# A planned kernel is planned anew: other model constants, five instead of six float32 heads kept, another order

## Chip, core and metric

The kernel runs on one core of a Trainium2 chip. The core has five engines with a queue of instructions each, worked off in order: PE (TensorE, matrix products into PSUM), DVE (VectorE), ACT (ScalarE), POOL (GpSimd) and SP (SyncE, which here only issues transfers). The metric is the time of one execution on the device in microseconds; of several runs the median counts.

## What is computed

Attention in hash buckets, and a feed-forward layer on its output. The reference, cut:

```python
# q, k, v: (4, 8, 768, 64) float32; proj: (64, 6)
q_bucket = np.sum(q_bits * powers, axis=-1)      # q_bits = (q @ proj > 0), k the same
mask = q_bucket[:, :, :, None] == k_bucket[:, :, None, :]
scores = scale * np.matmul(q, k.transpose(0, 1, 3, 2))
scores = np.where(mask, scores, -1000000000.0)
attn = np.exp(scores - np.max(scores, axis=-1, keepdims=True))
attn = attn / (np.sum(attn, axis=-1, keepdims=True) + 1e-09)
x = np.matmul(attn, v)           # to (3072, 512): rows are batch and position
h = x @ w_in                     # (512, 2048)
g = 0.5 * h * (1.0 + erf(h * inv_sqrt2))
return g @ w_out                 # (2048, 512)
```

The host hands over w_in and w_out as 64-bit words (doubles), which the kernel decodes to float32 itself.

## The kernel before

**Work.** The attention is cut into units: one head and 128 query rows against all 768 keys, 192 units in all. Batch 0 is done in two passes, `FIRST`: the first 256 rows of all eight heads (two units a head), then the other 512 (four units a head). Batches 1 to 3 are one pass each.

**A head in float32** (`head_plain`, L915, for all heads of the first pass): q and k of the head are loaded together (L921, 384 KB) into a set of tiles, k is moved to the other partitions, a projection on PE (L936) and the signs on ACT (L942) give the bucket bits, and four small copies (mask steps) write them beside q and k, so that the product of scores includes the mask. Scores are then two float32 products a unit, each run as two instructions (L987, x4).

**A head in split float16** (`head`, L617, for all other heads that aren't kept): load into `raw` (L627), maximum on DVE (L630), scale of the head (L587 to L605), high part (L460 or L464), moves of it (L643, on any engine or as a transfer), low parts (L661 on DVE, or L464 and L486 on POOL), projection (L695), signs (L701), masks. Scores are four float16 products a unit (L989, L990).

**Kept heads.** The first pass has eight sets of tiles (`NKEEP` = 6 and `NEARLY` = 2). After each pass of the loop the owners of sets from `AGAIN` = 6 on are dropped; a head whose set still has its owner is used again in the second pass as it stands, in float32. Sets 4 and 5 lie in memory that later holds x of other row chunks (`x` in the tile names, and `rest`).

**Behind the scores.** A unit goes on with the row maximum (L993, DVE), a guard and a shift (L998, L464 or L460), the exponential (L1007, ACT), and in batch 0 transposes on PE (L1069) and copies of them; then the product with v (L1152 in float32, L1161 split). `v_first` (L851) is v of batch 0 in three pieces. The feed-forward part uses split float16: hidden products (L1396), their evacuation (L1406), gelu (L1434), split (L460 or L464, and L1448), output products (L1478), drain (L1508), store (L1521). The weights come in 16 loads each for w_in and w_out (L745, three buffers `wraw`, first come first served in the order of creation: w_in before w_out), each followed by three decoding operations on DVE (L752, L757, L762), products for the scale (L775), and scaling and splitting. A hidden product needs the scales of all of w_in.

**The order.** No engine's order is written out by hand. Every piece of work is a step with an engine (or several to choose from), an estimated cost, needs, a key, and perhaps a ring of buffers from which it takes a slot. `Plan.order` (L126) simulates the engines with these costs. Whenever an engine is free, it takes the step with the lowest key (plus a summand for the engine, from `PAR`) among those that are ready in the simulation. Steps are then emitted in the order of their simulated starts, and the engines run them in that order, whenever they really become ready. Keys are a running unit number t minus or plus a number of `PAR`: the load of a head has t - H (the entry of the head, H0 to H7 in the first pass, G0 to G7 in the second) - HQ, v of batch 0 has VS0, a load of w_in has in0 to in3 plus a step - Lin, one of w_out the same with out. SP takes a simulated 0.65 us for an issue; `dma_at` says when the simulated transfers are through.

**PE's clock in the plan** (L239 to L251). The plan keeps PE's busy share by windows of 3.413 us. It begins with `warm` false; while it isn't warm, each PE step costs double. **Blanks** (`add_blank`, L415) are 128 spare steps of four products that nobody uses (L419, planned at 0.22 us for the four). A blank is taken only when no other PE step is ready, and not while the share of the last window is over `FILL` = 0.85:

```python
full = share > self.FILL
...
if s.spare and full:
    continue
```

Of the kernel before, what the change touches and what calls it, by code (L numbers as in the profile page):

```python
# [24 lines left out]
FIRST = (((0, 256),), ((256, 256), (512, 256)))  # L25
NEARLY = 2
PLAIN = (8, 0)
AGAIN = 6
BARE = False
WHOLE = (4, 4, 0, 0, 0)  # L30
TABLE = 1.3
# [4 lines left out]
GROW = ("p","hl")  # L36

PAR = dict(
    STICK=-82.49, LP_DVE=168.72, LP_Pool=131.55, KM=22.79, KM_ACT=-0.38, KM_DVE=21.62, KM_Pool=77.76, RN=-228.07,
    RT=-120.93, RC_ACT=-187.97, RC_DVE=104.4, XH_ACT=-169.94, XH_DVE=-58.71, XH_Pool=153.81, XL_DVE=2.29,  # L40
    XL_Pool=-84.29, VB=75.91, GU_DVE=376.97, GU_Pool=-283.34, SH_DVE=-141.74, SH_ACT=169, SH_Pool=-102.03,
    SF_DVE=106.59, SF_ACT=-91.62, SF_Pool=-105.46, SU=255.56, NM_DVE=139.91, NM_ACT=-81.24, NM_Pool=114.06,
    NM_SP=-82.67, NL_DVE=426.56, NL_Pool=109.97, NK_DVE=140.93, NK_ACT=118.24, NK_Pool=-152.1, Z=-98.92, VS0=-226.8,
    H0=1350.75, HL=-150.29, VS=-186.92, G2=45.62, HQ=-153.69, VQ=-322.44, in0=210.99, out0=-154.22, in1=106.47,
    out1=18.08, in2=-133.65, out2=-122.24, in3=462.36, out3=2.34, H1=390.62, H2=235.99, H3=74.68, H4=-91.19,
    H5=-484.96, H6=160.92, H7=182.63, MEV=-284.82, MGE=-95.53, MSP=-95.01, V0=-96.78, QK0=-173.32, QK1=188.62,
    QK2=101.09, MX0=117.31, MX1=-38.76, MX2=-22.52, EX0=-485.91, EX1=468.22, EX2=-110.13, NR0=17.49, NR1=108.73,
    NR2=80.71, HI0=-258.98, HI1=22.07, HI2=232.15, LO0=35, LO1=-160.32, LO2=2.65, PV0=-16.06, PV1=-698.65,
    PV2=-277.98, TR0=151.7, TR1=219.82, TR2=2.67, V1=-251.7, V2=66.98, Sin0=-94.82, Sin1=-40.21, Sin2=62.47,
    Sin3=-65.73, Sout0=12.07, Sout1=20.19, Sout2=-141.49, Sout3=15.82, Lin=572.06, Pin=97.32, Qin=138.76,  # L50
    Cin=-105.62, Min=-18.36, Lout=375.6, Pout=89.64, Qout=24.03, Cout=365.45, Mout=-620.71, G0=52.67, G1=-55.39,
    G3=17.42, G4=-204.1, G5=26.67, G6=177.05, G7=213.7, DUP0=-160.19, DUP1=-74.32, DUP2=842.69, LOW0=-36.13,
    LOW1=-187.95, LOW2=-265.14, PRJ0=293.66, PRJ1=118.05, PRJ2=248.42, MSK0=-16.31, MSK1=-34, MSK2=-4.17,
    DI_ACT=44.21, DI_DVE=54.03, DI_Pool=-87.05, WS_ACT=-12.67, WS_DVE=-97.95, WS_Pool=-164.14, WH_ACT=60.25,
    WH_DVE=76.08, WH_Pool=10.25, WL_ACT=-103.41, WL_DVE=147.58, WL_Pool=27.65, VH_ACT=90.01, VH_DVE=123.18,
    VH_Pool=-76.83, RND_ACT=-125.63, RND_DVE=144.01, RND_Pool=117.51, HI_ACT=-106.91, HI_DVE=738.91, HI_Pool=34.78,
    EV_ACT=28.16, EV_DVE=4.77, EV_Pool=-35.31, GH_ACT=-33.98, GH_DVE=180.18, GH_Pool=55.02, NS0=123.24, NS1=-168.39,
    NS2=409,
)
FULL = 65504.0  # L60
BIG = 2.0**34
# [19 lines left out]
class Plan:  # L81
# [19 lines left out]
    WINDOW = 3.413  # L101
    FILL = 0.85
    FALLS = 0.45
    FIRST_DMA = 2.4

    def __init__(self, rings):
        self.rings = {name: list(range(n)) for name, n in rings.items()}
# [2 lines left out]
    def add(self, engine, cost, emit, key, needs=(), takes=None, table=None, port=False, act=1.0, spare=False):  # L110
        s = Step(len(self.steps), engine, cost, emit, key, needs, takes, table, port, act, spare)
        self.steps.append(s)
        return s
# [12 lines left out]
    def order(self):  # L126
# [26 lines left out]
        free_at.update(self.START)  # L153
        dma_at, table, shape = self.FIRST_DMA, None, None
        port_at, port_of = 0.0, None
        warm, window, busy = False, 0, {}
        for t in set(free_at.values()):
            heapq.heappush(events, (t, -1, None))
        count, serial = 0, -1
# [1 line left out]
        while events and count < total:  # L161
            now, _, ended = heapq.heappop(events)
# [3 lines left out]
            for e in batch:  # L166
                if e is None:
                    continue
                if isinstance(e, dict):
                    self.rings[e["holder"].takes].append(e["holder"].slot)  # L170
                    continue
                for hold in e.frees:
                    hold["left"] -= 1
                    if not hold["left"]:
                        serial -= 1
                        late = self.LAG if hold["holder"].takes in self.PSUM else 0.0
                        heapq.heappush(events, (now + late, serial, hold))
                for u in users.get(e, ()):
                    left[u] -= 1
                    for w in u.ways:  # L180
                        hop = self.SAME.get(w, 0.05) if w == e.engine else self.HOP[e.engine] + self.INTO.get(w, 0.0)
                        at[u, w] = max(at.get((u, w), 0.0), now + hop)
                        if not left[u]:
                            heapq.heappush(events, (at[u, w], -1, None))
                    if not left[u]:
                        enlist(u)
            for engine, pool in ready.items():
                if free_at[engine] > now or not pool:
                    continue
# [42 lines left out]
                cost = s.cost  # L232
# [6 lines left out]
                if engine == "PE":  # L239

                    while window < int(now / self.WINDOW):
                        share = busy.get(window, 0.0) / self.WINDOW
                        warm = share > (self.FALLS if warm else 0.8)
# [7 lines left out]
                        a = b  # L251
                if engine == "SP":
                    free_at[engine] = now + 0.65
                    dma_at = max(dma_at, now + 1.0) + cost
                    if dma_at > now + self.QUEUE:
                        heapq.heappush(events, (dma_at - self.QUEUE, -1, None))
                    s.end = dma_at + 0.75
                else:
                    free_at[engine] = s.end = now + cost
                    if engine == "Pool" or (engine == "DVE" and s.port):  # L260
                        port_at, port_of = s.end - self.PORT, engine
                        heapq.heappush(events, (port_at, -1, None))
# [12 lines left out]
def tile_bucket_attention_moe(  # L275
# [136 lines left out]
    add, free = plan.add, plan.free  # L412
# [502 lines left out]
    def head_plain(b, h, i, key, clear, cl):  # L915

        both_of = pairs[i]
        rows_of = slice(0, D), slice(D, P)

        def load():  # L920
            nc.sync.dma_start(out=both_of[0], in_=qk[b, h])  # L921

        def move():
            affine(mv.engine, both_of[1][:D], both_of[0][D:])

        loaded = add("SP", 0.85, load, key - PAR["HQ"], clear)
        mv = add(affine_on("KM", S), 0, move, key + PAR["KM"], [loaded], port=True)
        space = add("none", 0, lambda: None, key, [loaded], takes="sign")
        HS = S // 2

        def project():
            for half in range(2):
                n = slice(half * HS, (half + 1) * HS)
                for k, rr in enumerate(rows_of):
                    r0 = half * 64 + k * 32
                    nc.tensor.matmul(  # L936
                        buf(pp)[r0 : r0 + 32, :HS], hash32[rr], both_of[0][rr, n], start=True, stop=True,
                        tile_position=(rr.start, r0),
                    )

        def sign():
            nc.scalar.activation(out=buf(space), in_=buf(pp)[:, :HS], func=AF.Sign, bias=off)  # L942

        pp = add("PE", 0.75, project, key + PAR[f"PRJ{cl}"], [space], takes="hp", table="quarter", act=0.5)
        sg = add("ACT", 0.1 + 0.833e-3 * HS + 0.186, sign, key + PAR[f"PRJ{cl}"], [pp, offs_ready])
        free(pp, [sg])
        masks = []
        rows = slice(D, D + 2 * NBIT)
        for half in range(2):
            for k, x in enumerate(both_of):  # L950
                box = []

                def mask(half=half, k=k, x=x, box=box):
                    r0 = half * 64 + k * 32
                    by = (BIG / 2, -BIG / 2) if k else (0.5, 0.5)
                    affine(
                        box[0].engine, x[rows, half * HS : (half + 1) * HS], buf(space)[r0 : r0 + 2 * NBIT], *by
                    )

                on = {  # L960
                    "DVE": (0.27, PAR["NK_DVE"]), "ACT": (0.53, PAR["NK_ACT"]), "Pool": (0.56, PAR["NK_Pool"])
                }
                box.append(add(on, 0, mask, key + PAR[f"MSK{cl}"], [sg] if k else [sg, mv], port=True))
# [606 lines left out]
```

## Time and profile before

| | us |
|---|---|
| median of 3 runs | 883.71 |
| lowest and highest | 882.57, 887.24 |
| the profiled execution | 884.62 |
| its span, from the first to the last instruction | 882.8 |
| PE busy in it | 861.6 |
| DVE, ACT, POOL busy | 668.3, 626.8, 404.9 |

The profile is of one execution. A row of a timeline gives start, duration, engine, line, operation, output and inputs, the count of instructions, and in brackets the idle time of the engine before it with what ended it. "Idle" of PE doesn't show where blanks run: these count as busy. The granted clock is the share of full speed at which PE was let run.

The share of PE's clock and the traffic of transfers over the span, in 40 slices of 22 us, the first slices at the left:

```profile
DMA  9652475116888697768675969586866593000000
GB/s 326 191 157 70 141 210 140 41 48 134 151 154 168 142 189 156 149 135 175 127 162 110 212 130 186 107 178 129 153 123 117 99 185 55 25 1 25 1 26 24
```

The first slice moves 326 GB/s, twice what most of the others do.

### The profile page before, as it was taken

To read this page: it belongs to the slowest core of one execution; us is meant where nothing else is said; L and a number is where in the kernel's file an instruction comes from. 1 tells how busy PE (TensorE), PEld (TensorE's weight loads), DVE (VectorE), ACT (ScalarE), POOL (GpSimd) and SP (SyncE) were. 2 spreads that over 40 slices of the span, in tenths; PEclk is the share of its full clock that TensorE was granted. 3 is DMA by queue.
4 is the path that set the end of the run, shared out by engine and by line. 5 is a ranking of instruction groups with operands and counts; after the bars stand their busy time and mean duration, and the time that the engine had idled before them with its cause. 6 is when DMAs were issued, how large, how long until landed. Compare 5 with 4: busy or idle time off the path is not lost. (4 is left out here: it accounts for less than half of the span.)

```text
span 882.8 us, 17207 instructions
## 1 busy us (share of the span) xinstructions
PE 861.6 (98%) x6419; PEld 554.4 (63%) x6419; DVE 668.3 (76%) x1360; ACT 626.8 (71%) x1061; POOL 404.9 (46%) x524
## 2 busy tenths in 40 slices
PE   7999988999999999999999999999999999999998
PEld 4666565666747656657656656665666566676663
DVE  5888888898898998998887988889887883212122
ACT  3788767898888887988797977887886773222221
POOL 2367545676667656656373655454553230000000
PEclk6999999999999999999999999999999999999999
DMA  9652475116888697768675969586866593000000
GB/s 326 191 157 70 141 210 140 41 48 134 151 154 168 142 189 156 149 135 175 127 162 110 212 130 186 107 178 129 153 123 117 99 185 55 25 1 25 1 26 24
DMA packets 281955, 111.48 MB, mean 126 GB/s; under 512 B 228624, under 2 KB 269584, under 8 KB 281872
## 3 DMA queue, kind: packets, MB, share of 16 engines
q1 hardware_dynamic: 281568, 110.39, 57.3%
q8 instruction: 50, 0.82, 0.4%
q14 instruction: 33, 0.27, 0.1%
q10 hardware_dynamic: 304, 0.00, 0.0%
HBM read 42.73 MB, written 6.29 MB: 56 GB/s over the span
## 5 line engine op out<-in xcount | busy, mean ns | idle before, releaser
L1396 PE MATMUL hp<-x,Win 128*128 128x256 f16 x2304 | 268.0, 272 | 0.5 <-ACT h L1406 0.2
L1478 PE MATMUL hp<-Wout,g 128*128 128x512 f16 x1152 | 263.3, 379 | 0.0
L1396 PEld LDWEIGHTS <-Win 128*128 128x128 f16 x2304 | 223.7, 98 | 41.6 <-issue 5.4
L993 DVE TENSOR_REDUCE rows<-s 128x1 f32<-128x768 f32 x192 | 180.7, 949 | 17.5 <-PE s L987 8.4
L1478 PEld LDWEIGHTS <-g 128*128 128x128 f16 x1152 | 110.8, 98 | 124.6 <-issue 4.1
L1007 ACT ACTIVATE p<-s,rows 128x768 f32<-128x768 f32 x141 | 139.2, 988 | 19.6 <-POOL rows L464 12.7
L1406 ACT ACTIVATE h<-hp,ffs 128x512 f32<-128x512 f32 x96 | 65.4, 681 | 89.5 <-PE hp L1396 87.9
L989 PE MATMUL s<-Q 88*128 88x384 f16 x304 | 99.4, 327 | 3.9 <-ACT wraw L1007 2.0
L990 PE MATMUL s<-K 128*128 128x384 f16 x304 | 99.2, 326 | 0.0
L464 DVE TENSOR_SCALAR g<-h,ffs 128x512 f16<-128x512 f32 x29 | 15.3, 526 | 96.0 <-ACT h L1434 68.3
L1448 DVE SCALAR_TENSOR_TENSOR g<-h,ffs,g 128x512 f16<-128x512 f32 x96 | 77.8, 822 | 6.6 <-ACT g L460 4.2
L998 POOL TENSOR_SCALAR rows<-rows,hs 128x1 f32<-128x1 f32 x68 | 48.1, 708 | 75.0 <-DVE rows L993 60.9
L486 POOL TENSOR_TENSOR K<-raw,Q 64x768 f16<-64x768 f32 x41 | 73.5, 1793 | 3.4
L1161 PE MATMUL hp<-pt,vhl 128*64 128x512 f16 (+1 forms) x864 | 74.9, 327 | 0.2 <-ACT h L1406 0.2
L1025 DVE SCALAR_TENSOR_TENSOR hl<-p,rows,hl 128x768 f16<-128x768 f32 x60 | 62.7, 1046 | 3.8 <-ACT hl L460 3.8
L1161 PEld LDWEIGHTS <-vhl 128*64 128x64 f16 x864 | 47.8, 110 | 25.4 <-issue 7.3
L1007 ACT ACTIVATE wraw<-s,rows 128x768 f32<-128x768 f32 x51 | 50.3, 985 | 12.0 <-POOL rows L464 7.1
L464 POOL TENSOR_SCALAR Q<-sign 24x384 f16<-24x384 f16 (+1 forms) x59 | 38.4, 651 | 36.6 <-ACT sign L701 13.4
L464 POOL TENSOR_SCALAR rows<-rows 128x1 f32<-128x1 f32 x87 | 31.9, 367 | 45.9 <-ACT p L1007 32.8
L464 POOL TENSOR_SCALAR raw<-raw,hs 64x768 f32<-64x768 f32 x41 | 44.0, 1072 | 5.8 <-ACT Q L460 2.3
L1434 ACT ACTIVATE h<-h 128x2048 f32<-128x2048 f32 x24 | 45.9, 1911 | 0.4
L989 PEld LDWEIGHTS <-Q 88*128 88x128 f16 x304 | 29.7, 98 | 25.0 <-issue 6.9
(169 smaller groups left out, 1302.5 us busy)
## 6 DMA issues: line engine op xcount, KB each, us to landing
raw<-qk SPq DMA_DIRECT2D x26, 384.0 KB, 3.6
vraw<-v SPq DMA_DIRECT2D x24, 384.0 KB, 4.1
wraw<-w_in SPq DMA_DIRECT2D x16, 512.0 KB, 4.5
wraw<-w_out SPq DMA_DIRECT2D x16, 512.0 KB, 4.1
out<-o SPq DMA_DIRECT2D x11, 512.0 KB, 3.5
K<-Q SPq DMA_DIRECT2D x28, 96.0 KB, 2.8
Q<-qk SPq DMA_DIRECT2D x6, 384.0 KB, 8.2
Q<-Q SPq DMA_DIRECT2D x20, 96.0 KB, 2.7
```

The lines of the kernel that those rows point to most:

```text
L464: on.tensor_scalar(out=o, in0=x, scalar1=scale, scalar2=bias, op0=ALU.mult, op1=ALU.add)
L486: on.tensor_tensor(out=o, in0=x, in1=y, op=ALU.subtract)
L989: nc.tensor.matmul(to, aq[kk, qs], ak[kk, n], start=True, stop=False)
L990: nc.tensor.matmul(to, bq[:, qs], bk[:, n], start=False, stop=True)
L993: nc.vector.tensor_reduce(out=nm, in_=both(sp), axis=AX.XY, op=ALU.max, negate=True)
L1007: nc.scalar.activation(out=buf(ex).rearrange("p (b k) -> p b k", b=2), in_=both(sp), func=AF.Exp, scale=sc, bias=nb, accum_out=ssum,)
L1025: nc.vector.scalar_tensor_tensor(out=buf(hi)[:, 1], in0=buf(ex), scalar=r, in1=buf(hi)[:, 0], op0=ALU.mult, op1=ALU.subtract,)
L1161: nc.tensor.matmul(pv[j * D : (j + 1) * D], buf(vh)[:, tv, kt, j * D : (j + 1) * D], pt_all[:, slots(j), tp * KT + kt], start=kt == 0 and ...
L1396: nc.tensor.matmul(buf(pair[0])[:, j * ch[1] : (j + 1) * ch[1]], win_hl[:, f0 // WB1, tw, pr, f0 % WB1 : f0 % WB1 + P], x[:, tx, pr, : ch[1]],
L1406: nc.scalar.activation(out=values_of()[:, 2 * fp : 2 * fp + 2, :nt], in_=buf(pair[0])[:, : 2 * nt].rearrange("p (j k) -> p j k", j=2), fun ...
L1448: nc.vector.scalar_tensor_tensor(out=gt[:, 1, s2, :nt], in0=h[:, s2, :nt], scalar=sg, in1=gt[:, 0, s2, :nt], op0=ALU.mult, op1=ALU.subtract,)
L1478: nc.tensor.matmul(buf(banks[u]).rearrange("p (c f) -> p c f", c=NWB), gt[:, tg, f, u * P : (u + 1) * P], wout_hl[:, :, tw, ft], start=ft ...
```

## The change

Five things are changed; the computation itself stays, apart from the way in which one head's scores are computed in the second pass.

1. `AGAIN` is 5: head 5 isn't kept after the first pass. It is loaded again in the second one and built in split float16 by `head`, as heads 6 and 7 are.
2. All numbers of `PAR` are others, so the whole order is another.
3. The plan starts with `warm` true, and for the first 25 us (`START_UP`) a blank may be taken at any share of the window.
4. After 220 us (`CALM`), a step of PE that needs a result of another engine counts as ready 0.4 us later in the plan (`SLACK`).
5. Transfers in the plan start at 2.2 instead of 2.4 us (`FIRST_DMA`), count 1.4 times while `dma_at` is below 10 us, and a float32 head's load is planned at 0.95 instead of 0.85.

```diff
-AGAIN = 6
+AGAIN = 5
...
-    NM_SP=-82.67, NL_DVE=426.56, NL_Pool=109.97, NK_DVE=140.93, NK_ACT=118.24, NK_Pool=-152.1, Z=-98.92, VS0=-226.8,
-    H0=1350.75, HL=-150.29, VS=-186.92, G2=45.62, HQ=-153.69, VQ=-322.44, in0=210.99, out0=-154.22, in1=106.47,
-    out1=18.08, in2=-133.65, out2=-122.24, in3=462.36, out3=2.34, H1=390.62, H2=235.99, H3=74.68, H4=-91.19,
-    H5=-484.96, H6=160.92, H7=182.63, MEV=-284.82, MGE=-95.53, MSP=-95.01, V0=-96.78, QK0=-173.32, QK1=188.62,
-    Sin3=-65.73, Sout0=12.07, Sout1=20.19, Sout2=-141.49, Sout3=15.82, Lin=572.06, Pin=97.32, Qin=138.76,
+    SF_DVE=114.89, SF_ACT=22.9, SF_Pool=67.26, SU=-74.96, NM_DVE=27.97, NM_ACT=589.06, NM_Pool=60.18, NM_SP=250.45,
+    NL_DVE=-89.75, NL_Pool=473.96, NK_DVE=348.41, NK_ACT=294.77, NK_Pool=753.57, Z=-138.1, VS0=-119.84, H0=900.94,
+    HL=2.46, VS=-383.82, G2=32.81, HQ=-101.13, VQ=-1915.59, in0=437.89, out0=298.78, in1=212.43, out1=-41.16,
+    in2=359.75, out2=-368.74, in3=-122.21, out3=190.56, H1=580.82, H2=108.46, H3=82.78, H4=-35.05, H5=-176.91,
+    H6=-395.11, H7=-340.05, MEV=231.41, MGE=65.81, MSP=181.72, V0=-1.96, QK0=243.97, QK1=-98.21, QK2=-236.57,
+    Sout0=-87.3, Sout1=419.51, Sout2=200.57, Sout3=-497.47, Lin=-705.32, Pin=-443.76, Qin=-491.14, Cin=-270.34,
+    G4=38.04, G5=-76.27, G6=52.19, G7=-329.08, DUP0=79.16, DUP1=237.67, DUP2=98.09, LOW0=-68.66, LOW1=44.7,
...
-    FIRST_DMA = 2.4
+    START_UP = 25.0
+    CALM = 220.0
+    SLACK = 0.4
+    FIRST_DMA = 2.2
...
-        warm, window, busy = False, 0, {}
+        warm, window, busy = True, 0, {}
...
                         hop = self.SAME.get(w, 0.05) if w == e.engine else self.HOP[e.engine] + self.INTO.get(w, 0.0)
+                        if w == "PE" and w != e.engine and now > self.CALM:
+                            hop += self.SLACK
...
-                    full = share > self.FILL
+                    full = share > self.FILL and now > self.START_UP
...
-                    dma_at = max(dma_at, now + 1.0) + cost
+                    dma_at = max(dma_at, now + 1.0) + cost * (1.4 if dma_at < 10.0 else 1.0)
...
-        loaded = add("SP", 0.85, load, key - PAR["HQ"], clear)
+        loaded = add("SP", 0.95, load, key - PAR["HQ"], clear)
```

More of the change, by code (lines that the diff above doesn't have):

```diff
@@ L38 @@
 PAR = dict(
[L39 to L42, printed above, removed]
-    NM_SP=-82.67, NL_DVE=426.56, NL_Pool=109.97, NK_DVE=140.93, NK_ACT=118.24, NK_Pool=-152.1, Z=-98.92, VS0=-226.8,
@@ L44 @@
-    H0=1350.75, HL=-150.29, VS=-186.92, G2=45.62, HQ=-153.69, VQ=-322.44, in0=210.99, out0=-154.22, in1=106.47,
-    out1=18.08, in2=-133.65, out2=-122.24, in3=462.36, out3=2.34, H1=390.62, H2=235.99, H3=74.68, H4=-91.19,
-    H5=-484.96, H6=160.92, H7=182.63, MEV=-284.82, MGE=-95.53, MSP=-95.01, V0=-96.78, QK0=-173.32, QK1=188.62,
-    QK2=101.09, MX0=117.31, MX1=-38.76, MX2=-22.52, EX0=-485.91, EX1=468.22, EX2=-110.13, NR0=17.49, NR1=108.73,
-    NR2=80.71, HI0=-258.98, HI1=22.07, HI2=232.15, LO0=35, LO1=-160.32, LO2=2.65, PV0=-16.06, PV1=-698.65,
@@ L49 @@
-    PV2=-277.98, TR0=151.7, TR1=219.82, TR2=2.67, V1=-251.7, V2=66.98, Sin0=-94.82, Sin1=-40.21, Sin2=62.47,
-    Sin3=-65.73, Sout0=12.07, Sout1=20.19, Sout2=-141.49, Sout3=15.82, Lin=572.06, Pin=97.32, Qin=138.76,
-    Cin=-105.62, Min=-18.36, Lout=375.6, Pout=89.64, Qout=24.03, Cout=365.45, Mout=-620.71, G0=52.67, G1=-55.39,
-    G3=17.42, G4=-204.1, G5=26.67, G6=177.05, G7=213.7, DUP0=-160.19, DUP1=-74.32, DUP2=842.69, LOW0=-36.13,
-    LOW1=-187.95, LOW2=-265.14, PRJ0=293.66, PRJ1=118.05, PRJ2=248.42, MSK0=-16.31, MSK1=-34, MSK2=-4.17,
@@ L54 @@
[L54 to L58, printed above, removed]
+    STICK=-43.82, LP_DVE=252.11, LP_Pool=251.88, KM=-23.47, KM_ACT=53.26, KM_DVE=19.8, KM_Pool=14.44, RN=285.08,
@@ new lines @@
+    RT=-473.64, RC_ACT=366.88, RC_DVE=-15.69, XH_ACT=-59.57, XH_DVE=-219.59, XH_Pool=-211.94, XL_DVE=35.95,
+    XL_Pool=42.57, VB=-37.18, GU_DVE=-18.1, GU_Pool=145.48, SH_DVE=310.56, SH_ACT=236.82, SH_Pool=-7.15,
+    SF_DVE=114.89, SF_ACT=22.9, SF_Pool=67.26, SU=-74.96, NM_DVE=27.97, NM_ACT=589.06, NM_Pool=60.18, NM_SP=250.45,
+    NL_DVE=-89.75, NL_Pool=473.96, NK_DVE=348.41, NK_ACT=294.77, NK_Pool=753.57, Z=-138.1, VS0=-119.84, H0=900.94,
+    HL=2.46, VS=-383.82, G2=32.81, HQ=-101.13, VQ=-1915.59, in0=437.89, out0=298.78, in1=212.43, out1=-41.16,
@@ new lines @@
+    in2=359.75, out2=-368.74, in3=-122.21, out3=190.56, H1=580.82, H2=108.46, H3=82.78, H4=-35.05, H5=-176.91,
+    H6=-395.11, H7=-340.05, MEV=231.41, MGE=65.81, MSP=181.72, V0=-1.96, QK0=243.97, QK1=-98.21, QK2=-236.57,
+    MX0=-75.02, MX1=-54.32, MX2=97.52, EX0=-439.08, EX1=241.39, EX2=578.47, NR0=26.53, NR1=45.56, NR2=34.07,
+    HI0=11.5, HI1=-129.04, HI2=163.39, LO0=145.39, LO1=100.73, LO2=-114.72, PV0=67.27, PV1=-168.87, PV2=199.4,
+    TR0=-80.53, TR1=-564.81, TR2=-53.7, V1=-46.37, V2=-45.25, Sin0=180.81, Sin1=-790.65, Sin2=175.27, Sin3=145.52,
@@ new lines @@
+    Sout0=-87.3, Sout1=419.51, Sout2=200.57, Sout3=-497.47, Lin=-705.32, Pin=-443.76, Qin=-491.14, Cin=-270.34,
+    Min=-310.31, Lout=57.28, Pout=31.21, Qout=117.23, Cout=233.59, Mout=68.2, G0=172.25, G1=61.83, G3=92.77,
+    G4=38.04, G5=-76.27, G6=52.19, G7=-329.08, DUP0=79.16, DUP1=237.67, DUP2=98.09, LOW0=-68.66, LOW1=44.7,
+    LOW2=-1040.47, PRJ0=-83.56, PRJ1=68.33, PRJ2=92.55, MSK0=-608.85, MSK1=300.29, MSK2=134.22, DI_ACT=48.74,
+    DI_DVE=127.83, DI_Pool=-157.92, WS_ACT=235.62, WS_DVE=532.58, WS_Pool=143.4, WH_ACT=393.38, WH_DVE=39.84,
@@ L59 @@
+    WH_Pool=112.27, WL_ACT=18.05, WL_DVE=-198.45, WL_Pool=150.66, VH_ACT=-223.21, VH_DVE=-110.78, VH_Pool=-64.33,
+    RND_ACT=237.94, RND_DVE=153.55, RND_Pool=40.29, HI_ACT=-141.09, HI_DVE=174.64, HI_Pool=-280.03, EV_ACT=-334.83,
+    EV_DVE=1273.48, EV_Pool=-145.54, GH_ACT=92.39, GH_DVE=402.64, GH_Pool=-92.12, NS0=-256.91, NS1=-16.95,
+    NS2=544.56,
 )
```

## The prediction

> **What bounds the kernel now.** I read the head of the page first, to see whether one engine fills the span, and then how the share runs over time.
>
> ```profile
> span 882.8 us, 17207 instructions
> PE 861.6 (98%) x6419; PEld 554.4 (63%) x6419; DVE 668.3 (76%) x1360; ACT 626.8 (71%) x1061; POOL 404.9 (46%) x524
> ```
>
> TensorE is busy for 861.6 of 882.8 us, so the kernel is bound by it, and only 21.2 us of plain idle time are left. DVE (VectorE) comes next with 76%. A mean hides stages, so next the table of windows, cut where the character of the work changes: start, attention with weight decoding, the change-over to the feed-forward part, the long steady mix, the tail.
>
> ```profile
> 0.00:30.00 30.00, 23.69 (x163) 16.43 (x164) 16.74 (x41) 10.24 (x17) 8.50 (x28) 0.72 0.94 326
> 30.00:100.00 70.00, 68.82 (x521) 44.67 (x520) 62.89 (x137) 60.40 (x117) 44.36 (x70) 1.00 0.40 120
> 100.00:160.00 60.00, 54.83 (x409) 34.59 (x409) 52.91 (x116) 42.40 (x85) 30.08 (x44) 1.00 0.55 153
> 160.00:220.00 60.00, 59.04 (x472) 40.00 (x471) 54.53 (x129) 53.62 (x95) 42.53 (x55) 1.00 0.34 78
> 220.00:700.00 480.00, 475.90 (x3626) 303.25 (x3625) 420.08 (x840) 396.56 (x663) 269.16 (x313) 1.00 0.76 150
> 700.00:884.00 184.00, 179.31 (x1236) 115.45 (x1234) 61.16 (x101) 63.62 (x88) 10.29 (x16) 1.00 0.19 41
> ```
>
> Columns: window, its length, busy PE, weight load, DVE, ACT, POOL, granted clock, DMA share, GB/s. From 220 us on PE misses 4.1 us in 480, and then the ending. A new order can win back no more than that there. Before 220 us PE misses 6.3 + 1.2 + 5.2 + 1.0 = 13.7 us, and its busy time isn't all work: blanks are in it.
>
> ```profile
> L419 PE MATMUL hp<-blank 128*128 128x128 bf16 x224 | 19.6, 254 | 3.0 <-DVE hash L402 1.0 <-DVE both_offs L545 0.6 <-ACT sign L701 0.6
> ```
>
> These are up to 19.6 us, so up to 33 us of PE's first 220 are not work. That is the pot. What keeps PE from filling it is the supply from DVE: 62.9 of 70 us busy from 30 to 100, 52.9 of 60 from 100 to 160. DVE's own idle time in 30 to 220 is 7.1 + 7.1 + 5.5 = 19.7 us, scattered. In the start it is 13.3 of 30. Now the start itself, PE's timeline.
>
> ```profile
> 0.98 3.42 PE L419 MATMUL hp<-blank 128*128 128x128 bf16 x32 [0.98 <-DVE hash L402]
> 6.32 0.85 PE L936 MATMUL hp<-Q,hash 64*32 64x384 f32 x8 [1.93 <-DVE hash L409]
> 9.93 0.19 PE L542 MATMUL hp<-offs,shift 128*128 128x1 bf16 x2 [2.75 <-DVE offs L538]
> ...
> 12.93 2.90 PE L987 MATMUL s<-K,Q 76*128 76x384 f32 x4
> 15.76 1.51 PE L936 MATMUL hp<-Q,hash 64*32 64x384 f32 x8
> 17.19 2.93 PE L987 MATMUL s<-K,Q 76*128 76x384 f32 x4
> ...
> 20.77 3.98 PE L419 MATMUL hp<-blank 128*128 128x128 bf16 x36
> 24.68 0.85 PE L936 MATMUL hp<-Q,hash 64*32 64x384 f32 x8
> ...
> 26.14 1.51 PE L987 MATMUL s<-K,Q 76*128 76x384 f32 x4
> ```
>
> One L987 x4 is the scores of one unit (128 query rows). Two units run by 20 us, at 2.9 us each, the third one at 26.14 in 1.51. The shorter ones are at full clock; the windows say which clock was granted.
>
> ```profile
> 10.00:15.00 5.00, 4.35 (x27) 3.22 (x26) 4.90 (x14) 2.46 (x4) 0.58 (x1) 0.50 1.05 403
> 15.00:20.00 5.00, 5.00 (x15) 1.61 (x14) 4.57 (x9) 1.69 (x4) 1.52 (x4) 0.50 1.05 399
> 20.00:25.00 5.00, 5.00 (x49) 4.70 (x51) 3.30 (x6) 1.01 (x2) 2.11 (x3) 0.54 1.06 370
> 25.00:30.00 5.00, 5.00 (x40) 3.34 (x33) 3.18 (x7) 2.95 (x6) 1.71 (x4) 1.00 1.00 304
> ```
>
> So from 10 to about 24.5 us the clock is 0.50, the transfers fill the DMA engines (share 1.05), and ACT, which has the exponentials, is busy 1.0 to 2.5 us in 5. The start is short of heads, not of PE.
>
> **The change part by part.**
>
> *Order of the first transfers.* The plan issues what is ready with the lowest key. With the old numbers that gives h0, three pieces of w_in, h1, v, h2, h7, h6, and SP does just that:
>
> ```profile
> 0.73 0.40 SPq L921 DMA_DIRECT2D Q<-qk  x1
> 1.19 1.51 SPq L745 DMA_DIRECT2D wraw<-w_in  x3
> 2.75 0.51 SPq L921 DMA_DIRECT2D Q<-qk  x1
> 4.23 3.02 SPq L851 DMA_DIRECT2D v_first<-v  x3
> 9.71 1.29 SPq L921 DMA_DIRECT2D Q<-qk  x3
> ...
> 14.76 0.33 SPq L921 DMA_DIRECT2D Q<-qk  x1
> ```
>
> Since my hand calculation of the keys agrees with the queue, I trust it for the new numbers. A head's load has start - H + (-HQ): h0 0 - 900.9 + 101.1 = -800; h1 2 - 580.8 + 101.1 = -478; v (VS0) -120; h2 -3, h3 24, h4 144, raw of h5 213, then h6's, h5 288, h7 455, h6 508. The first w_in pieces have in0 - Lin = 437.9 + 705.3 = 1143. So the change sends all heads and v ahead of the weights. The sizes are in the list of issues:
>
> ```profile
> wraw<-w_in SPq DMA_DIRECT2D x16, 512.0 KB, 4.5
> ...
> Q<-qk SPq DMA_DIRECT2D x6, 384.0 KB, 8.2
> ```
>
> Up to the third head that takes 3 x 512 KB = 1.57 MB out of the way: at the 403 GB/s of the row 10 to 15, 3.9 us. For the fourth (h3, now issued at 14.76 behind h7, h6, a fourth w_in and two raw) it is 3.6 MB, 9 us. Heads come 4 to 9 us sooner.
>
> *Clock and blanks.* With blanks allowed in every gap of the first 25 us, the stretch from 12.93 to 20 could run at full clock. Its three pieces took 2.90 + 1.51 + 2.93 = 7.3 us. The same kinds at clock 1.00 are 1.51 and 0.85 above: 1.51 + 0.85 + 1.51 = 3.9. That is 3.5 us of PE time. What doesn't go away: PE is in order and its L542 waits for the 0.5 KB of offsets until 9.93, and the first sign and mask steps come after it. So the first unit stays near 12.9 us. A price on the other side: 32 blanks took 3.42 us, 0.43 for four, where the plan books 0.22. If PE starts with the 16 blanks that fit in the plan until the first projection (from 1.1 to 4.6 us), they take 16 x 0.43 = 6.9 us at the slow rate, to 7.9, and delay the projection at 6.32 by 1.6; this is hidden as long as the offsets hold L542 until 9.93, and PE idles there anyway.
>
> The Trainium skill ("TensorE: Matmul & The Clock Gate", Part 1) says that one busy window of about 3.4 us brings the full clock and about one idle window takes it. The trace agrees on the fall and not on the rise: PE is busy 5.00 of 5.00 us from 15 to 20 at 0.50, and the clock comes back only behind the 3.98 us of blanks. By the rule the 3.5 us would be won as soon as no gap is left; by the trace the float32 work can let the clock fall again between two runs of blanks, and then nothing of it is won.
>
> *What the start is worth.* The units are ahead by 26.14 - 17 = 9 us at the most: the mask inputs of the second head follow the projection at 15.76, so its scores could stand at about 17. DVE, however, spent 10 to 16 us of the start on decoding w_in; this work only moves back. DVE's idle time from 10 to 30 us is 0.10 + 0.43 + 1.70 + 1.82 = 4.05 us, and because DVE is what feeds the stage until 220 us, this is what is kept if units fill it. Ends: 0 (all of it swallowed by DVE later) and -9 (the whole lead is kept). I take -5: the 4 us of the DVE row, and 1 more of the clock's 3.5, most of which PE would only have waited.
>
> *One head fewer is kept.* In the second pass (512 rows, four units a head) head 5 is built anew in split float16.
>
> ```profile
> 74.56 2.75 PE L987 MATMUL s<-K,Q 76*128 76x384 f32 x8
> 77.15 0.82 PE L1069 MATMUL hp<-ident,p 128*128 128x128 f32 x6
> ...
> 301.63 0.33 PE L989 MATMUL s<-Q 88*128 88x384 f16 x1
> ...
> 302.29 4.09 PE L1396 MATMUL hp<-x,Win 128*128 128x256 f16 x36
> ```
>
> Two float32 units run from 74.56 to 77.15, 1.30 each; one split unit from 301.63 to 302.29, 0.66. Four units: -2.6 us of PE. Against it one projection and the small products:
>
> ```profile
> L695 PE MATMUL hp<-K,hash 128*32 128x384 f16 x208 | 13.2, 331 | 0.2 <-ACT h L1406 0.2
> L630 DVE TENSOR_REDUCE tops<-raw 128x1 bf16<-128x768 f32 x26 | 24.6, 945 | 0.7 <-DMA raw<-qk 0.3
> L596 DVE TENSOR_SCALAR hs<-hs 128x2 f32<-128x2 f32 x26 | 6.0, 249 | 0.0
> L486 POOL TENSOR_TENSOR K<-raw,Q 64x768 f16<-64x768 f32 x41 | 73.5, 1793 | 3.4
> ```
>
> L695 is 8 instructions a head, 13.2 / 26 = 0.5 us. Net PE: -2.1. DVE gets the maximum, 0.95, and four small scale steps, of which the row of 0.25 is the longest: at most 1.9 us. POOL gets the two subtractions of the low parts, 2 x 1.79 = 3.6 us, with their scalings and the masks at most 8 (as much again, an estimate from that row), in a stage where it is busy 30 of 60 us; ACT, busy 42 of 60, gets the sign and the high part. A 384 KB load and the moves on SP lie in a stage with a DMA share of 0.55. So these are covered; without cover, four units wait those 8 us once. As DVE feeds this stage, the ends are -2.1 (PE's saving counts) and +1.9 (DVE's addition counts); I take -1: PE's saving is given back only where DVE is the last, and DVE has 7.1 us free in the window 100 to 160.
>
> *Slack for PE behind other engines, after 220 us.* It moves PE work so that a late ACT or DVE result is waited for less. PE's idle time there is the 4.1 us of the row 220 to 700. Ends -4 and, if the new order is worse in the same amount, +4; I take -1.5. From 700 us on nothing changes.
>
> Sum: -5 - 1 - 1.5 = -7.5 us on the profiled execution's 884.6 us (span 882.8 and 1.8 around it) is 877.1. The profiled run lies 0.9 above the median 883.71, so the forecast is **876.2**, and I say 876.5.
>
> **The rivals.**
>
> *The lead is kept whole.* The heads' 9 us in the start are not lost again, because the decode work fills DVE's 19.7 scattered idle us. For it: those idle us. Against it: DVE would have to run at more than 95% from 30 to 220. 883.7 - 9 - 2 = 872; 866 to 873.
>
> *Nothing that can be measured.* The start gains, but DVE's work before the feed-forward products can begin is the same plus 1.9 us, and PE waits for it later instead; or the clock stays at 0.50 in the start, since the plan's full clock is counted, not granted. Then 880 to 887, about 883.
>
> *The weights come late (slower).* PE is saturated only once the feed-forward products can run, and these need all of w_in decoded, scaled and split.
>
> ```profile
> L762 DVE SCALAR_TENSOR_TENSOR Win<-wraw,Win x4: 678/682/686, 86.6 to 110.3; 128x512 int32<-128x512 int32 x4
> ```
>
> ```profile
> 157.18 1.47 PE L1396 MATMUL hp<-x,Win 128*128 128x256 f16 x12
> ```
>
> The last w_in decode is at 110.3 and the first product at 157.18. The change puts eight heads, v and the raw of h5 and of h6 ahead of the first w_in: 10 x 384 + 3 x 512 KB = 5.5 MB, 13.7 us at 403 GB/s, against one head now (0.4 MB, 1 us). So w_in begins about 12 us later. If the decoding stays late by that much, and the chain behind it as well, the first product comes at about 169 and PE idles for most of the difference, for it has little else in that stage: 884 + 12 - 1 = 895. It decides when the first L1396 is more than 4.4 us later than 157.18. Against it: sixteen pieces of w_in need some 20 us of transfers at that rate, yet the last one is decoded at 110.3. So in the old order DVE's turn and the buffers set that time, not the start of the transfers.
>
> **How the numbers follow.** About 0.5% (4.4 us: below 879.3 or above 888.1) is what a measurement of this kernel can tell from no change. Forecast, 873 to 879.3: 0.45. Lead kept whole, up to 873: 0.15. Nothing measurable: 0.26. Weights late: 0.14. So faster 0.60, same 0.26, slower 0.14. The range 867 to 887 leaves out the late weights, the top of the unmeasurable and a little below 867, about 0.19.
>
> **What would show it.** Right: SP's first issues are heads and v without w_in; granted clock above 0.75 as a mean of 10 to 25 us; the third unit's scores before 20 us; four or more units by 26; L987 with 144 instead of 160 instructions and L989 with 320 instead of 304; the first L1396 before 155; PE idle and blanks before 220 us together under 28 us. Wrong: the clock at 0.50 until 24; the first L1396 after 160; in 220 to 700 more than 6 us of idle PE. The forecast falls if DVE's share from 30 to 160 doesn't rise, or if the lead of the start is gone by 100 us.

## The result, and the profile after

The changed kernel takes 889.48 us, median of ten runs (886.13 to 894.94), against 883.65 us (879.72 to 887.24) of the kernel before on the same chip. The ratio is 1.0067 with a 95% interval of 1.0048 to 1.0087: slower, by some 6 us. The profiled execution took 889.63 us. In the changed file every line of the prediction stands five lines further down (L1396 is L1401, L989 is L994, L1007 is L1012).

The head of its page, and then its table of windows, cut as in the prediction:

```profile
span 887.8 us, 17388 instructions
...
PE 861.9 (97%) x6501; PEld 554.3 (62%) x6501; DVE 683.2 (77%) x1358; ACT 618.3 (70%) x1056; POOL 393.6 (44%) x521
```

```profile
0.00:30.00 30.00, 27.42 (x275) 20.01 (x276) 18.92 (x52) 15.37 (x28) 10.84 (x33) 1.00 0.84 290
30.00:100.00 70.00, 67.19 (x522) 44.63 (x521) 66.94 (x137) 51.36 (x107) 36.59 (x59) 1.00 0.52 156
100.00:160.00 60.00, 59.29 (x460) 39.06 (x459) 53.21 (x108) 45.12 (x92) 33.01 (x46) 1.00 0.52 146
160.00:220.00 60.00, 54.13 (x423) 33.84 (x422) 52.52 (x116) 53.04 (x91) 47.98 (x56) 1.00 0.28 60
220.00:700.00 480.00, 469.48 (x3560) 297.65 (x3557) 423.30 (x833) 388.11 (x651) 249.43 (x307) 1.00 0.75 149
700.00:889.00 189.00, 184.41 (x1274) 119.09 (x1272) 68.31 (x116) 65.32 (x94) 15.72 (x22) 0.99 0.20 44
```

The span is 5.0 us longer. PE's busy time is the same within 0.3 us, so nearly all of it is idle time of PE, and a subtraction of the busy column from the length, row by row, says where. Before and after: 6.3 and 2.6 in the start, 1.2 and 2.8 from 30 to 100, 5.2 and 0.7 from 100 to 160, 1.0 and 5.9 from 160 to 220, 4.1 and 10.5 from 220 to 700. Up to 160 us the new order has idled 6.6 us less. From 160 to 220 it loses 4.9 of them, and from 220 to 700 another 6.4.

**The start went as planned.** SP's queue of the changed kernel:

```profile
0.73 0.88 SPq L926 DMA_DIRECT2D Q<-qk  x2
1.66 1.57 SPq L856 DMA_DIRECT2D v_first<-v  x3
4.29 1.69 SPq L926 DMA_DIRECT2D Q<-qk  x2
...
13.76 2.87 SPq L750 DMA_DIRECT2D wraw<-w_in  x3
```

PE's timeline there:

```profile
12.84 2.85 PE L992 MATMUL s<-K,Q 76*128 76x384 f32 x8
15.53 2.85 PE L424 MATMUL hp<-blank 128*128 128x128 bf16 x48
18.30 0.85 PE L941 MATMUL hp<-Q,hash 64*32 64x384 f32 x8
...
20.27 1.51 PE L992 MATMUL s<-K,Q 76*128 76x384 f32 x4
```

Heads and v come first, w_in after 13 us. The scores of two units stand at 12.84 in 2.85 us together; before, each took 2.9. The third unit comes at 20.27 where it came at 26.14.

**What the lead was used for.** The lists of instructions by line give the first and the last start of each group (in us, behind the min, median and max duration in ns):

```profile
L767 DVE SCALAR_TENSOR_TENSOR Win<-wraw,Win x16: 660/681/694, 30.4 to 81.7; 128x512 int32<-128x512 int32 x16
...
L491 POOL TENSOR_TENSOR Wout<-o,Wout x16: 664/672/1272, 176.7 to 206.2; 128x256 f16<-128x256 f32 x16
...
L1401 PE MATMUL hp<-x,Win x2304: 269/273/283, 98.3 to 865.6; 128*128 128x256 f16 x192
...
L1483 PE MATMUL hp<-Wout,g x1152: 376/379/631, 209.8 to 883.6; 128*128 128x512 f16 x192
```

The output products of the kernel before:

```profile
L1478 PE MATMUL hp<-Wout,g x1152: 376/379/390, 204.5 to 878.5; 128*128 128x512 f16 x192
```

The hidden products begin at 98.3 us, 59 us sooner than the 157.18 of before. But the first output product comes at 209.8, 5.3 later. And attention is hardly ahead. Counted by the exponentials on ACT, the third unit starts at 26.7 us instead of 29.5, but the 24th at 101.0 against 100.3 before, and the 48th at 187.5 against 188.4. DVE did fill its gaps (66.94 busy us from 30 to 100 instead of 62.89). Up to 100 us it did some 3 us more each for w_in and for the heads that are built in split float16, not for more units: both orders have begun 23 exponentials by then. So in 100 to 160 us PE filled its gaps with hidden products that it would have done later. From 160 to 196 it had too little to go on with: 5.8 of the 5.9 idle us lie there, and from 196 to 220 it idles 0.07 us. At 220 us the new order has begun 204 hidden products, 30 output products and 55 exponentials, the old one 192, 20 and 56. Of its lead 3.6 us of products were left, and it was one unit behind.

### The profile page after: what moved, and what is told of

It is laid out like the page before. It is cut to its first block, busy times and chain, and to the rows that moved or that the text cites. A ratio compares the mean times of both kernels' runs of the same rounds, so it can differ in the third digit from the quotient of the medians.

```text
span 887.8 us, 17388 instructions
## 1 busy us (share of the span) xinstructions
PE 861.9 (97%) x6501; PEld 554.3 (62%) x6501; DVE 683.2 (77%) x1358; ACT 618.3 (70%) x1056; POOL 393.6 (44%) x521
## 4 chain that ended last, share of the span: by engine, by line
PE 54%; DVE 14%; ACT 6%; issue 4%; DMA 3%; POOL 1%; ACTq 0%; DVEq 0%; POOLq 0%; SPq 0%
PE hp L1483 20%; PE hp L1401 19%; PE hp L1166 6%; DVE rows L998 4%; PE s L994 4%; PE s L995 3%; DVE hl L1030 3%; DMA pt<-hl 2%; DVE K L666 1%; ACT p L1012 1%; PE hp L1157 1%; ACT wraw L1012 1%; DVE g L1453 1%; DVE wraw L1030 1%; PE hp L700 1%
## 5 line engine op out<-in xcount | busy, mean ns | idle before, releaser
L1401 PE MATMUL hp<-x,Win 128*128 128x256 f16 x2304 | 267.2, 272 | 3.5 <-DVE pt L469 1.6
L1401 PEld LDWEIGHTS <-Win 128*128 128x128 f16 x2304 | 224.2, 98 | 43.6 <-issue 7.0
L1012 ACT ACTIVATE p<-s,rows 128x768 f32<-128x768 f32 x142 | 140.3, 989 | 24.1 <-POOL rows L469 10.0
L994 PE MATMUL s<-Q 88*128 88x384 f16 x304 | 99.7, 328 | 10.2 <-ACT p L1012 5.0
L1003 POOL TENSOR_SCALAR rows<-rows,hs 128x1 f32<-128x1 f32 x77 | 50.1, 650 | 94.9 <-DVE rows L998 84.9
L1030 DVE SCALAR_TENSOR_TENSOR hl<-p,rows,hl 128x768 f16<-128x768 f32 x80 | 84.3, 1059 | 8.8 <-ACT hl L465 4.1
L469 DVE TENSOR_SCALAR g<-h,ffs 128x512 f16<-128x512 f32 x25 | 12.9, 517 | 85.7 <-ACT h L1439 63.4
L1453 DVE SCALAR_TENSOR_TENSOR g<-h,ffs,g 128x512 f16<-128x512 f32 x96 | 74.9, 795 | 4.0 <-ACT g L465 1.8
L469 POOL TENSOR_SCALAR rows<-rows 128x1 f32<-128x1 f32 x96 | 40.9, 426 | 45.5 <-DVE rows L1003 15.4
L1012 ACT ACTIVATE wraw<-s,rows 128x768 f32<-128x768 f32 x50 | 49.3, 986 | 8.1 <-DVE rows L1021 3.2
L491 POOL TENSOR_TENSOR K<-raw,Q 64x768 f16<-64x768 f32 x27 | 50.7, 1878 | 2.3
L465 ACT ACTIVATE hl<-p,rows 128x768 f16<-128x768 f32 x38 | 35.3, 929 | 23.5 <-DMA pt<-hl 6.8
L995 PEld LDWEIGHTS <-K 128*128 128x128 f16 x304 | 29.8, 98 | 31.0 <-issue 14.5
L469 POOL TENSOR_SCALAR Q<-sign 24x384 f16<-24x384 f16 (+1 forms) x54 | 32.7, 606 | 35.1 <-ACT sign L947 9.8
L994 PEld LDWEIGHTS <-Q 88*128 88x128 f16 x304 | 29.8, 98 | 26.3 <-issue 9.5
```

Of the source, the lines that this page charges most:

```text
L469: on.tensor_scalar(out=o, in0=x, scalar1=scale, scalar2=bias, op0=ALU.mult, op1=ALU.add)
L491: on.tensor_tensor(out=o, in0=x, in1=y, op=ALU.subtract)
L994: nc.tensor.matmul(to, aq[kk, qs], ak[kk, n], start=True, stop=False)
L995: nc.tensor.matmul(to, bq[:, qs], bk[:, n], start=False, stop=True)
L1012: nc.scalar.activation(out=buf(ex).rearrange("p (b k) -> p b k", b=2), in_=both(sp), func=AF.Exp, scale=sc, bias=nb, accum_out=ssum,)
L1030: nc.vector.scalar_tensor_tensor(out=buf(hi)[:, 1], in0=buf(ex), scalar=r, in1=buf(hi)[:, 0], op0=ALU.mult, op1=ALU.subtract,)
```

## The experiments

Two places need a cause: the 6.4 us between 220 and 700, and the start's lead that brings nothing. The first question is whether the late idle time belongs to the order or to one execution.

**The changed kernel again (x0_after).** No edit.

> The changed kernel again, for a second profile. Theory 'order': the slip against its own plan between 540 and 700 us (PE idle there some 7 us, against 2 in the kernel before) belongs to this order and comes again, at the same units, within 2 us. Rival 'chance': it was a late transfer in one execution; then PE idle in 540 to 700 is 2 to 4 us this time and the total some 4 us shorter, 885.

It took 892.17 us (886.16 to 893.79), ratio 1.0087 (1.0060 to 1.0115). One row of the windows each, 540 to 720 us. The changed kernel as profiled first:

```profile
540.00:720.00 180.00, 173.65 (x1284) 107.48 (x1283) 152.99 (x286) 136.56 (x232) 81.72 (x101) 0.99 0.68 128
```

Again, in this run:

```profile
540.00:720.00 180.00, 173.55 (x1295) 108.07 (x1294) 153.77 (x289) 138.19 (x234) 81.25 (x101) 1.00 0.69 130
```

The kernel before:

```profile
540.00:720.00 180.00, 178.71 (x1359) 112.60 (x1357) 156.78 (x293) 147.40 (x248) 85.18 (x108) 1.00 0.73 138
```

6.35 and 6.45 us of idle PE, against 1.29. It belongs to the order. Most of it (6.2 and 6.3 us) are waits of the scores (L994) for an exponential (L1012). The longest, 2.36 us, leads to a cause. PE's timeline:

```profile
688.85 1.46 PE L1483 MATMUL hp<-Wout,g 128*128 128x512 f16 x6
692.67 0.48 PE L994 MATMUL s<-Q 88*128 88x384 f16 x1 [2.36 <-ACT wraw L1012]
...
693.90 2.42 PE L1483 MATMUL hp<-Wout,g 128*128 128x512 f16 x6
```

ACT's timeline:

```profile
690.71 0.94 ACT L465 ACTIVATE hl<-p,rows 128x768 f16<-128x768 f32 x1 [4.68 <-DVE rows L469]
691.55 0.97 ACT L1012 ACTIVATE wraw<-s,rows 128x768 f32<-128x768 f32 x1
```

SP's queue:

```profile
684.85 1.43 SPq L1037 DMA_TRANSPOSE pt<-hl  x1
688.26 5.95 SPq L1037 DMA_TRANSPOSE pt<-hl  x2
```

PE waits for the exponential at 691.55. That stands behind ACT's L465, which writes the high part of another unit's weights into a buffer `hl` and has stood still for 4.68 us. The profile names DVE, the releaser that came last by its reckoning. But `hl` is a ring: two tiles of its own and, once w_out is decoded, one of the `wraw` tiles. Each is written (L465 or L469 the high part, L1030 the low part), then transposed by a transfer (L1037) into `pt`, and can be taken again when that has landed. The theory is therefore 'buffers': ACT waits for an `hl` that a transfer still reads. By the list of DMA issues a transfer takes 4.1 us in the median, and the three out of `hl` from 682 to 697 us took up to 5.4:

```profile
pt<-hl SPq DMA_TRANSPOSE x96, 4.1
```

```profile
L1037 SPq DMA_TRANSPOSE pt<-hl x3: 1433/1443/3214, 684.8 to 692.8; - x3
...
DMA to landing us min/median/max: 3.9/5.3/5.4
```

The longest is the one issued at 684.85. It lands at 690.3, and L465 starts 0.4 us behind that, at 690.71.

**A fourth `hl` buffer, in the new order (x2_hl4_after) and in the old one (x3_hl4_before).** The third `wraw` tile is used as well. Slots are dealt again behind the planning, so that the order of all instructions stays:

```diff
     steps = plan.order()
+    bufs["hl"].append(bufs["wraw"][2][:, :S].bitcast(F16).rearrange("p (t k) -> p t k", t=2))
+    ready_at = max(s.end for s in w_read)
+    freed = {0: 0.0, 1: 0.0}
+    for s in steps:
+        if s.takes != "hl":
+            continue
+        if s.start > ready_at and len(freed) == 2:
+            freed.update({2: ready_at, 3: ready_at})
+        s.slot = min(freed, key=lambda k: (freed[k], k))
+        freed[s.slot] = max(f.end for f in plan.let_go[s])
```

> The changed kernel with a fourth hl buffer (the third wraw tile, free once the weights are decoded), slots dealt anew behind the planning, the order of each engine as it was. Theory 'buffers' (ACT and POOL wait for an hl buffer that a transposing transfer still reads, and PE then for ACT): PE idle in 540 to 720 falls from 9 to under 5 us, the total by 3 to 6 us, to 884 to 886. Rival 'order of ACT' (PE waits for an exponential that is late in ACT's own queue for other reasons): under 1.5 us.

> The kernel before with the same fourth hl buffer, order unchanged. Theory 'buffers': it has 2 us of PE idle in 540 to 720 to win, so 0 to -2 us. Rival: no difference, within 1 us of 883.7.

The new order with four buffers took 881.86 us (878.32 to 886.72), ratio to the kernel before 0.9981 (0.9953 to 1.0009). Its window:

```profile
540.00:720.00 180.00, 179.10 (x1373) 114.75 (x1372) 157.21 (x302) 141.59 (x241) 87.16 (x108) 1.00 0.73 136
```

The old order with four took 880.97 us (878.11 to 882.82), ratio 0.9974 (0.9956 to 0.9993):

```profile
540.00:720.00 180.00, 179.89 (x1373) 114.06 (x1372) 157.95 (x296) 149.15 (x251) 85.22 (x107) 1.00 0.74 141
```

The idle time falls from 6.4 to 0.9 us in the new order and from 1.3 to 0.1 in the old one, and the time by 8 to 10 us in the new, 2.5 in the old. 'Buffers' holds, and both orders hang on the ring. In the new order it is worth more than the idle time in that window. The half clock behind the long wait goes too, which cost some 1.5 us there: four products of the scores and six output products fill 3.49 us from 692.67 on, and the same ten take 1.97 in the kernel before (from 203.81). The rest wasn't followed up. The median of x2_hl4_after also hides the clock: at a mean granted clock of 0.999 or more it took 878.32 to 879.83 us, at 0.992 to 0.994 it took 883.90 to 886.72.

With four buffers in both, the new order (881.86) is no faster than the old one (880.97). So the ring accounts for the loss, and not for the missing gain.

**Two `hl` buffers in the old order (x9_hl2_before)**, the same edit without the new slots. The order was planned for three. With two, 135 of 152 takings of a slot start in the plan before the last reading of that slot's previous unit has ended, so that engines must wait. Of these, 26 stand in the order even ahead of that reading. There the old contents are overwritten before they are read, some units multiply v with another unit's weights, and the waits aren't those of two buffers.

> The kernel before with two hl buffers instead of three, the order of the steps unchanged, only the slots dealt again. 'Buffers' (a late hl buffer is what the time after 460 us hangs on): waits for hl come into the old order too; idle time of PE from 540 to 720 us rises from 1.3 to over 4 us, median 887 to 893. Rival ('order': the old order doesn't need the third buffer, the waits of the new one come from its steps): idle time there stays under 2.5 us, median within 2 us of 883.4.

It took 995.48 us, with 24.9 us of idle PE from 540 to 720. That is far more than either theory gave, and for the reason just told it can't be read as the price of the third buffer. The run settles nothing; x3_hl4_before carries the point for the old order.

**Half clock in the start of the new order (x1_one_product).** A blank is one product instead of four:

```diff
-            for k in range(4):
+            for k in range(1):
```

> The changed kernel with one product in each blank instead of four; its order is the same. Theory 'supply' (until the first output product, near 210 us, the pace is that of DVE, ACT and POOL): the clock stays at 0.50 for much of the first 30 us, the lead of PE there shrinks by up to 4 us, but the first L1483 stays within 1.5 us of 209.8 and the total within 2 us of 889.5. Rival 'clock': what the full clock won in the start is kept to the end; the total rises by 3 to 4 us, to 893.

It took 896.86 us (896.51 to 897.30), ratio 1.0156 (1.0130 to 1.0182). PE's timeline of the start:

```profile
11.84 5.49 PE L992 MATMUL s<-K,Q 76*128 76x384 f32 x8
...
21.02 1.51 PE L992 MATMUL s<-K,Q 76*128 76x384 f32 x4
```

The first two units take 5.49 instead of 2.85 us, which is the half clock. Yet the third comes at 21.02, 0.75 us later than with it full. What the run lost, it lost elsewhere, as the windows say:

```profile
85.00:90.00 5.00, 2.95 (x22) 1.95 (x20) 4.76 (x15) 4.78 (x9) 4.50 (x7) 0.92 0.37 111
90.00:95.00 5.00, 5.00 (x14) 3.20 (x13) 2.92 (x6) 3.30 (x5) 3.01 (x4) 0.50 0.25 61
95.00:100.00 5.00, 4.56 (x20) 3.05 (x19) 3.78 (x6) 3.51 (x6) 1.16 (x1) 0.50 0.00 0
100.00:105.00 5.00, 5.00 (x21) 2.63 (x20) 3.63 (x12) 3.29 (x6) 2.72 (x4) 0.50 0.26 79
```

From 89 to 109 us the clock is halved again (the changed kernel has blanks there too, which are smaller here), and PE is nearly full while DVE, ACT and POOL fall to some 3 of 5 us. In the start the half clock is nearly hidden, here it isn't. The first output product comes at 221.2 us instead of 209.8, so both expectations failed: 'supply' had it within 1.5 us, and 'clock' had the total at 893. The run tells little of the start's worth, since it touched both places.

**Full clock in the start of the old order, with four buffers (x5_hl4_blanks) and with three (x1b_before_more).** The first twelve blanks have eight products, all else stays as in x3_hl4_before or in the kernel before:

```diff
-    def add_blank():
+    def add_blank(n):
...
-            for k in range(4):
+            for k in range(8 if n < 12 else 4):
```

> The kernel before with the fourth hl buffer and eight products instead of four in its first twelve blanks, order unchanged. If the half clock of the start costs the end (rival 'clock'), 3 to 4 us less than with the buffer alone (880.97), 877. If only DVE, ACT and POOL set the pace there (theory 'supply'), within 1.5 us of 881, though the mean clock of the first 30 us rises from 0.77 to over 0.9.

> The kernel before with eight instead of four products in the first twelve blanks, order and buffers unchanged. 'Clock in the start' (the full clock from about 4 us on is worth what the pair with a fourth buffer showed): granted clock from 0 to 30 us up from 0.72 to over 0.9, first hidden product at 152 to 154 instead of 157.2, median 2 to 3 us under the kernel before, 880.5 to 881.5. Rival (it was worth something only together with the fourth buffer): median 882.5 to 884, first hidden product earlier by under 2 us or the lead gone by 460 us.

With four buffers: 878.54 us (877.63 to 879.10), ratio 0.9945 (0.9931 to 0.9960). This is the best version of all and beats both kernels. Its lists by line:

```profile
L1398 PE MATMUL hp<-x,Win x2304: 269/273/283, 152.4 to 853.9; 128*128 128x256 f16 x192
...
L1480 PE MATMUL hp<-Wout,g x1152: 376/379/390, 199.7 to 871.9; 128*128 128x512 f16 x192
```

The hidden products of x3_hl4_before, the same without the blanks:

```profile
L1398 PE MATMUL hp<-x,Win x2304: 269/273/283, 156.8 to 857.3; 128*128 128x256 f16 x192
```

So the full clock brings the first hidden product 4.4 us forward and the median time 2.4 us down, nearer to the rival 'clock' (3 to 4) than to 'supply' (under 1.5). The two versions weren't run side by side; against the kernel before, the intervals of their ratios just touch.

This run also tells what the order of the transfers is worth in the start. It still issues three pieces of w_in behind the first head, as the kernel before does, and PE's timeline has the scores of its third unit here:

```profile
19.39 1.56 PE L989 MATMUL s<-K,Q 76*128 76x384 f32 x4
```

That is 19.39 us, against 24.06 in x3_hl4_before, 26.14 in the kernel before and 20.27 in the changed one. The full clock alone brings the third unit as far forward as the whole change does; with three buffers (the next run) it stands at 20.32.

With three buffers: 884.50 us (883.26 to 888.24), ratio 1.0014 (0.9996 to 1.0032), so nothing, although the lead is there too. Its lists by line:

```profile
L1396 PE MATMUL hp<-x,Win x2304: 269/273/283, 154.2 to 862.0; 128*128 128x256 f16 x192
...
L1478 PE MATMUL hp<-Wout,g x1152: 376/379/390, 201.5 to 880.0; 128*128 128x512 f16 x192
```

And its windows:

```profile
220.00:460.00 240.00, 234.91 (x1773) 146.71 (x1768) 209.41 (x424) 200.62 (x333) 145.00 (x167) 1.00 0.76 151
460.00:700.00 240.00, 236.88 (x1808) 153.84 (x1807) 206.56 (x411) 191.76 (x326) 117.29 (x143) 1.00 0.74 146
```

The first output product is 3.0 us ahead of the 204.5 of before and the last one 1.5 behind its 878.5. From 220 to 700 us PE idles 8.2 us in the profiled execution (886.15 us, so 1.65 above the median), against 4.1. A lead of 3 us at 200 us is lost behind it, and with the fourth buffer it isn't: the medians with three buffers are 883.5 to 883.9 (the kernel before) and 884.5 without and with the full clock, with four they are 881.0 and 878.5. The expectation that the lead would stay failed, and its rival holds.

**Without one of three decoding operations on w_out (x4_no_wout_op).** Does DVE's decoding keep the output products back from 160 to 220 us? The kernel leaves out L767 for w_out, so w_out loses its low bits.

```diff
-                    else:
+                    elif name == "in":
```

> The changed kernel without the third decoding operation of w_out (L767 on Wout, 16 x 0.68 = 11 us of DVE between 100 and 166 us are left out, so w_out lacks its low bits); the order is the same. Theory 'supply': DVE's turn sets the pace until w_out is split; the first L1483 comes 4 to 10 us before 209.8 and the total falls by 4 to 8 us against the changed kernel (890 to 892 so far). Rival 'PE or ACT sets it': the first L1483 moves by under 2 us and the total by under 2.

It took 887.49 us (884.78 to 892.99), ratio 1.0059 (1.0030 to 1.0089):

```profile
L1483 PE MATMUL hp<-Wout,g x1152: 376/379/390, 211.0 to 878.8; 128*128 128x512 f16 x192
```

11.7 us less of DVE's work, and the output products begin at 211.0, not sooner. The rival holds: DVE's decoding isn't what is late there.

**Without the slack (e2_noslack).** `SLACK = 0.0`, planned anew with the new numbers.

> The changed kernel planned with SLACK 0: the same order up to 220 us, another one behind it. Theory 'slack harms' (the later PE steps in the plan make this order the fragile one): PE idle in 540 to 720 falls under 3 us and the total by 4 us or more. Theory 'slack is neither here nor there' (the buffers make the waits, whatever the slack): idle in 220 to 720 stays at 6 to 14 us, the total within 3 us of the changed kernel, 888 to 895.

It took 888.55 us (884.07 to 894.06), ratio 1.0058 (1.0031 to 1.0084): as the changed kernel. PE idles 9.3 us from 220 to 700, so the slack neither makes nor cures the waits. It moves them: 2.8 us lie in 540 to 720, where the changed kernel has 6.4, and 5.5 in 220 to 460.

**Six heads kept (e1_keep6).** `AGAIN = 6`, planned anew with the new numbers.

> The changed kernel with six heads kept again, all else as it is, planned anew. The steps differ, so every key meets another queue. Theory 'the order is found for one set of steps': 10 us slower or more than the changed kernel, over 900, and this says nothing of the head itself. Theory 'the head rebuilt costs DVE and POOL more than PE saves': faster than the changed kernel by 1 to 3 us.

One run: 905.15 us, as the theory had it by which the keys of `PAR` were found for one set of steps. The same keys on another set give another order, here a longer one. The run says nothing of what a kept head is worth.

## Why the prediction failed

The forecast was 876.5 us and faster; it came out slower at 889.48, above the range.

**The start, -5 us: the mechanism was right up to 30 us, the step from it to the end wrong.** The order of the transfers, the clock and the units came as said or nearly so: 1.00 granted in the start, four units by 26 us, the third at 20.27 (said: before 20). But the two causes don't add up there: the clock alone brings the third unit to 19.39 in x5_hl4_blanks. The step that failed is "this is what is kept if units fill it". DVE's gaps were filled, and not with units: by 100 us both orders have begun 23 exponentials. That is the prediction's own end of 0, "all of it swallowed by DVE later". What the new order did have ahead at 160 us were hidden products pulled forward, and most of that was given back from 160 to 196. In the old order, where the full clock can be had alone, a lead of 3 us reaches 200 us and is then lost (x1b_before_more). It is worth 2.4 us at the end once a fourth buffer lets it through (x5_hl4_blanks). So the clock's part of the term measured about nothing with three buffers; no run tries the order of the transfers by itself. My sign for this, idle time and blanks before 220 us under 28 us, came out at 12 + 22 = 34; in the old order these are 14 + 19 = 33.

**Slack, -1.5 us with ends at -4 and +4: the wrong thing was priced.** I looked at 220 to 700 us as a pot of 4.1 us from which a new order could win, and bounded its loss by the same 4.1. It lost 6.4 in idle time, and with the half clock behind the waits the ring costs it 8 to 10 us by x2_hl4_after, where it costs the old order 2.5 (x3_hl4_before). The cause is the ring `hl` and not the slack (e2_noslack). The prediction named no ring behind the scores. The profile of before had the hint in its waits: 1.1 of its 1.29 idle us from 540 to 720 were the scores waiting for exponentials, the same wait as here.

**One head fewer kept, -1 us: not settled.** The float32 scores went from 160 to 144 instructions, as said, and the split ones from 304 to 312. My 320 was a slip, since one head has four units with two such instructions each. Its share of the time can't be taken alone, as e1_keep6 shows.

**The rivals.** 'The lead is kept whole' is refuted: as many units have begun by 100 us as before, and PE idles 12 us up to 220. 'The weights come late' was wrong for w_in: its last decoding came at 81.7 us instead of 110.3, though its loads began 12 us later; this bears out the argument against it in the prediction, that the start of the transfers didn't set that time. 'Nothing that can be measured' had the half that is true, that PE waits later for what it gained, but it put the wait at the decoding and gave it no further loss.

**What stays open.** Why PE runs short from 160 to 196 us, and why the first output product comes 5 us late. PE doesn't stand still in front of it, so its order has it there. POOL's last split of w_out starts at 206.2 us, 3.6 before it, where the old order has 194.1 and 10.4, and POOL's 47.98 of 60 busy us from 160 to 220 are the highest share that it has in any stage; this was only read, not tried. And why the new order loses more at the ring than the old one. In the plans both rings are about as tight: 44 of 152 takings in the old order and 45 in the new one start at the very moment at which a slot comes free. The planners put the two orders at 881.3 and 881.8 us, and the spans are 882.8 and 887.8, so it is the new one that misses its plan. Both gain by a fourth buffer, and no run singles out the step of the order that makes the difference.

## What to carry to other kernels

Before a gain in an early stage is counted at the end, look for the ring with the least room in the stages behind it: a lead that arrives at a full ring turns into waits. Where an order is planned with buffers taken the moment they come free, a small pot of idle time isn't a bound on the loss of another order. And where an engine's idle time falls in one stage and rises in the next by as much (4.5 and 4.9 us here), count what has been begun by the end of the second: it tells how much of the work was only pulled forward.

## What the runs showed of the hardware

**The column of the granted clock can be wrong at the beginning.** For the start of x1_one_product it shows 1.00, while the same eight products took 5.49 us there and 2.85 in the changed kernel. Durations of equal instructions decide.

**PE can be busy and stay at half clock.** In x1_one_product it is busy 5.00 of 5.00 us from 90 to 95 and from 100 to 105, at 0.50, mostly with float32 scores (76 rows) and float32 transposes, and stays so for 20 us. The Trainium skill ("TensorE: Matmul & The Clock Gate", Part 1) gives the full clock after one busy window of about 3.4 us. By that rule it would have come back by 97 us; the trace disagrees, as it did in the start of the kernel before (5.00 of 5.00 us from 15 to 20, at 0.50).

**A wait of 2.36 us can cost the clock.** Behind it, at 692.67 us, the scores took 0.48 and 0.52 us instead of 0.33, and six output products 2.42 instead of 1.46. The same section of the Trainium skill has the clock fall after one idle window of about 3.4 us; here it fell with less idle time than that. The prediction counted the trace of before as agreeing on the fall. But the clock there had fallen by 7.50 us, and the longest idle stretch of PE since its first product was 1.93 us (before 6.32), so that trace doesn't show a whole idle window either.
